# A fused attention and token-mixing kernel: q and k share each load tile on the two partition halves, in longer rows

One Trainium2 chip, one core. The metric is the device time in microseconds (us) of one execution, median over runs. "DMA us" below means packet time summed over all records of the trace and divided by the 16 DMA engines of the core.

Terms: PE is TensorE (matmuls and transposes), DVE VectorE, ACT ScalarE, POOL GpSimd, and SP issues the DMAs. HBM is the chip's main memory, SBUF the on-chip memory of 128 partitions, PSUM the memory that PE writes to; an eviction copies from PSUM to SBUF. A packet is one DMA record of the trace, here one contiguous row (8,192 of 2,304 B for q and k before, 4,096 of 4,608 B after). A transfer is full height when it stands on 128 partitions, half height on 64. Clash is my word for something that the traces show and do not explain: with half-height transfers on partitions 0 to 63 or 64 to 127, packets can take clearly longer than others of their size. In the kernel before, the last pair of half-height stores took 127 ns a packet of 2,048 B on average, the full-height weight loads of that size 84.6 ns. I call such packets stretched, and packets near the median of full-height transfers undisturbed (84 ns for 2,048 B, 93 for 2,304 B). An engine's part of a transfer is taken as a sixteenth of its packets. A run counts as slow when it is over 1.5% above the fastest of its kernel; ratios leave slow runs out.

## The reference

Eight batches of 8 heads, 576 tokens, 64 values a head: attention with a causal window of 128 tokens and a bias linear in distance, then a token mixer on the concatenated heads.

```python
scores = q @ k.T / 8 + slopes[h] * -(i - j)        # kept where 0 <= i - j < 128
attn   = softmax(scores) @ v                       # 8 x 8 x 576 x 64
x      = heads concatenated                        # 8 x 576 x 512
wq, wk = x @ w_q, x @ w_k                          # 512 -> 64
mixed  = (wq @ wk.T / 8) @ x
out    = relu(mixed) @ w_out                       # fp32, 8 x 576 x 512
```

q, k and v are fp32 in HBM, 9.4 MB each.

## The kernel before

Every operation is a small record, and a string, PLAN, lists the operations in order with engine and PSUM bank. All DMAs are issued from SP on one queue. The parts that matter here:

```python
RINGS = {"ld": 8, ..., "qT": 4, "kT": 4, ..., "osb": 3, ...}
ld = [sb([P, 2, 576], FP32, f"ld{i}") for i in range(8)]           # 128 partitions, rows of 2,304 B

# per batch b, group f of four heads, x = q or k: one load of 576 KB over 128 partitions
nc.sync.dma_start(out=t, in_=srcs[x][b].rearrange(
    "(f i a) (g j) d -> f (a g) i (j d)", f=2, a=2, j=9)[f])
copy(eng, n, t.rearrange("p i (j d) -> p j i d", j=9))             # cast to fp16, mostly on POOL
for j in range(9):                                                 # transposes on PE
    for a in range(2):
        r = slice(64 * a, 64 * a + 64)
        nc.tensor.transpose(bank(bk[a])...[:, 64 * j : 64 * j + 64], n[r, j]..., ident[r, r])
copy(eng, dst.rearrange("p a (g j) -> p a g j", j=9),              # eviction to qT or kT, contiguous
     src.rearrange("p a (j g) -> p a g j", j=9))
...                                                                # [cut] scores, exp, bias, values, mixer
nc.sync.dma_start(out=out[b, P*(t-1) : P*(t+1), :].rearrange("(p t) d -> p t d", t=2),
                  in_=osb[n % 3])                                  # stores of two tiles, 512 KB
```

The softmax here doesn't subtract the row's maximum and nothing guards it: scores larger than these inputs give would overflow.

## Time and profile before

| | before |
|---|---|
| time, median (range), 4 runs | 151.48 us (150.78 to 153.2) |
| span of the profiled run, granted clock | 149.7 us, 1.00 |
| busy PE, DVE, ACT | 125.7, 125.7, 118.5 us |
| DMA us, all records | 134.3 |
| of it packets of q and k (8,192 of 2,304 B) | 58.2, mean 113.6 ns, median 93 |
| of it packets of 256 B (v and the two small weights, 37,888) | 46.8, mean 19.8 ns, median 18 |

The prediction shows the lines of the page, of the table by stretch, of the chain and of the waits. One view is added: the page's list of DMA issues, which gives for each kind count, KB and median us from issue to landing.

```profile
ld<-in_k_dram SPq DMA_DIRECT2D x16, 576.0 KB, 6.9
ld<-in_q_dram SPq DMA_DIRECT2D x16, 576.0 KB, 7.0
```

And the place where the input stage ends, in the timeline of PE (start us, length us): the last 18 transposes of q and k.

```profile
118.07 0.44 PE L159 MATMUL bank<-ident,nat 64*128 64x64 f16 x18
```

From there to the end of the span are 149.7 - 118.1 = 31.6 us.

### The profile page before, as it was taken

The page shows a single profiled execution, that of the slowest core. Times are in us where ns is not written, and L with a number is a line of the kernel's source. Part 1 is how long each engine was busy: PE and PEld are TensorE (multiplying, and loading weights), DVE is VectorE, ACT ScalarE, POOL GpSimd, SP SyncE. Part 2 cuts the span into 40 slices and gives each one's busy share as a digit, 9 for nine tenths or more (in the row PEclk, how much of TensorE's full clock was granted, in tenths as well). Part 3 has the DMA queues.
Part 4 walks back from the last instruction along what each step waited for, and adds up shares of the span by engine and source line. Part 5 has one row for each costly group of instructions (what it writes and reads, how often), then busy time and mean ns, then how long its engine had stood idle before and what let it go on. Part 6 is the DMA issues. An engine that isn't in the chain of part 4 may idle for free.

```text
span 149.7 us, 5314 instructions
## 1 busy us (share of the span) xinstructions
PE 125.7 (84%) x2308; PEld 82.6 (55%) x2308; DVE 125.7 (84%) x212; ACT 118.5 (79%) x170; POOL 58.9 (39%) x78
## 2 busy tenths in 40 slices
PE   6567388676889979889989999999789999999870
PEld 6465167555756456547466566576544757555320
DVE  5749987979999998789999989999799989994700
ACT  6959937995889868997799999959889989741560
POOL 4064137354915767333845381364341710000000
PEclk9999999999999999999999999999999999999999
DMA  4999999999999999999999999799699896033075
GB/s 151 383 327 266 180 365 351 264 171 358 389 263 191 296 299 195 236 306 309 348 348 372 338 405 227 167 254 279 157 371 340 235 385 222 4 140 144 0 314 176
DMA packets 50775, 39.40 MB, mean 263 GB/s; under 512 B 39488, under 2 KB 39488, under 8 KB 50752
## 3 DMA queue, kind: packets, MB, share of 16 engines
q1 hardware_dynamic: 50752, 39.07, 88.7%
q8 instruction: 18, 0.29, 0.8%
q14 instruction: 5, 0.04, 0.1%
HBM read 29.62 MB, written 9.44 MB: 261 GB/s over the span
## 4 chain that ended last, share of the span: by engine, by line
PE 40%; DMA 16%; DVE 13%; ACT 12%; SPq 9%; POOL 4%; issue 2%; POOLq 0%; DVEq 0%
PE bank L159 40%; DMA ld<-in_q_dram 10%; SPq L159 9%; ACT pt L159 8%; DMA ld<-in_k_dram 6%; DVE pt L159 5%; POOL nat L159 2%; ACT qT L159 2%; DVE xT L159 2%; POOL vt L159 2%; DVE x L159 2%; ACT kT L159 1%; DVE kT L159 1%; DVE osb L159 1%; DVE rm L159 1%
## 5 line engine op out<-in xcount | busy, mean ns | idle before, releaser
L159 ACT ACTIVATE pt<-bank 128x1024 f16<-128x1024 f32 x64 | 62.7, 1036 | 9.3 <-PE bank L159 9.0
L159 POOL CAST nat<-ld 128x1152 f16<-128x1152 f32 x30 | 34.2, 1146 | 36.7 <-PE bank L159 10.6
L159 DVE TENSOR_TENSOR pt<-pt,table 128x2048 f16<-128x2048 f16 x32 | 41.0, 1293 | 2.1 <-ACT pt L159 2.0
L159 PE MATMUL bank<-wout_sb,rm 128*128 128x512 f16 x128 | 31.8, 380 | 0.0
L159 POOL CAST vt<-ldv 128x512 f16<-128x512 f32 (+1 forms) x35 | 20.8, 613 | 25.4 <-DVE pt L159 15.5
L159 PE MATMUL bank<-qT,kT 64*128 64x256 f16 (+2 forms) x320 | 25.4, 267 | 4.6 <-ACT qT L159 2.0
L159 PE MATMUL bank<-vt,pt 128*128 128x65 f16 x576 | 23.7, 200 | 4.6 <-ACT pt L159 3.1
L159 PEld LDWEIGHTS <-pt 128*128 128x128 f16 x576 | 21.4, 102 | 9.7 <-issue 2.6
L159 DVE TENSOR_TENSOR x<-bank,inv 128x640 f16<-128x640 f32 x32 | 25.8, 817 | 0.8
L159 PEld LDWEIGHTS <-kT 64*128 64x128 f16 x320 | 14.5, 99 | 11.5 <-issue 8.6
L159 ACT COPY osb<-bank 128x512 f32<-128x512 f32 x24 | 13.9, 606 | 7.1 <-PE bank L159 7.1
L159 PE MATMUL bank<-ident,nat 64*128 64x64 f16 x576 | 14.7, 199 | 5.6 <-POOL nat L159 2.8
L159 PEld LDWEIGHTS <-nat 64*128 64x128 f16 x576 | 12.2, 100 | 10.1 <-POOL nat L159 4.7
L159 PEld LDWEIGHTS <-rm 128*128 128x128 f16 x128 | 10.8, 98 | 12.6 <-issue 2.5
L159 ACT COPY qT<-bank 128x1152 f16<-128x1152 f16 x12 | 13.5, 1121 | 2.6 <-PE bank L159 2.6
L159 ACT ACTIVATE rm<-bank 128x512 f16<-128x512 f32 x21 | 12.7, 610 | 2.2 <-PE bank L159 2.2
L159 DVE COPY kT<-bank 128x1152 f16<-128x1152 f16 x8 | 10.8, 1354 | 3.2 <-PE bank L159 3.2
L159 DVE COPY xT<-bank 128x640 f16<-128x640 f16 (+1 forms) x32 | 12.5, 448 | 0.4 <-PE bank L159 0.4
L159 PE MATMUL bank<-x,wkn 128*64 128x512 f16 x80 | 10.1, 383 | 0.0
L159 PE MATMUL bank<-wqT,gm 64*128 64x256 f16 x64 | 8.4, 288 | 1.5 <-DVE wqT L159 0.6
L159 ACT COPY kT<-bank 128x1152 f16<-128x1152 f16 x8 | 9.1, 1138 | 0.5 <-PE bank L159 0.5
L159 DVE TENSOR_SCALAR rm<-bank 128x512 f16<-128x512 f32 x11 | 7.5, 684 | 2.3 <-PE bank L159 2.2
(45 smaller groups left out, 112.1 us busy)
## 6 DMA issues: line engine op xcount, KB each, us to landing
ld<-in_k_dram SPq DMA_DIRECT2D x16, 576.0 KB, 6.9
ld<-in_q_dram SPq DMA_DIRECT2D x16, 576.0 KB, 7.0
ldv<-in_v_dram SPq DMA_DIRECT2D x32, 256.0 KB, 7.1
out_dram<-osb SPq DMA_DIRECT2D x16, 512.0 KB, 5.2
ldv<-in_v_dram SPq DMA_DIRECT2D x8, 128.0 KB, 7.3
osb<-in_moe_w_out_dram SPq DMA_DIRECT2D x2, 512.0 KB, 7.1
out_dram<-osbt SPq DMA_DIRECT2D x8, 128.0 KB, 3.8
osbt<-in_moe_w_q_dram SPq DMA_DIRECT2D x1, 128.0 KB, 5.3
```

The source lines that it names most:

```text
L159: r = call(*a, **k)
```

## The change

The intent: rows of 18 tokens (4,608 B) halve the packets of q and k. So that a transposed group still holds two heads on each partition column, q then needs 64 partitions only; q takes partitions 0 to 63 of a tile, k 64 to 127. Besides: the last batch stores tile by tile, a fourth output buffer, more evictions allowed on ACT, and a new PLAN.

```diff
-    ld = [sb([P, 2, 576], FP32, f"ld{i}") for i in range(RINGS["ld"])]     # 8
+    ld = [sb([P, 2, 1152], FP32, f"ld{i}") for i in range(RINGS["ld"])]    # 4
-                    nc.sync.dma_start(out=t, in_=srcs[x][b].rearrange(
-                        "(f i a) (g j) d -> f (a g) i (j d)", f=2, a=2, j=9)[f])
+                    nc.sync.dma_start(out=t[64 * x : 64 * x + 64], in_=srcs[x][b].rearrange(
+                        "(f i a) (g j) d -> f (a g) i (j d)", f=2, a=2, j=18)[f])
-                    copy(eng, n, t.rearrange("p i (j d) -> p j i d", j=9))
+                    copy(eng, n, t.rearrange("p i (h j d) -> p h j i d", h=2, j=9)[:, h])
-                    copy(eng, dst.rearrange("p a (g j) -> p a g j", j=9),
-                         src.rearrange("p a (j g) -> p a g j", j=9))
+                    dst = qkT[b % 2][:, f, :, :, 0:S].rearrange(
+                        "p x a (g h j) -> p x a g h j", h=2, j=9)[:, :, :, :, h]
+                    copy(eng, dst, src[:, :, 0:S].rearrange("p x (j a g) -> p x a g j", j=9, a=2))
...                                                       # [cut] reads of qT, kT become reads of qkT
-            op({"DVE": 0.74}, f"XTe{b}{c}", ...           # likewise WKe, WQe
+            op({"DVE": 0.74, "ACT": 1.05}, f"XTe{b}{c}", ...
-"osb": 3
+"osb": 4
+            if b == NB - 1:                               # last batch: one store of 256 KB per tile
+                    nc.sync.dma_start(out=out[b, P * t : P * t + P, :],
+                                      in_=osb[n % RINGS["osb"]][:, t % 2, :])
...                                                       # [cut] PLAN replaced as a whole
```

More of the change, by code (lines that the diff above doesn't have):

```diff
@@ L99 @@
 PLAN = """
-1G 6D 39S 4D 0G 35S 2D 7D 47S 3G 8P0 5D 43S 14P0 20A 65S 19A 11P0 23A 59S 18A 12P0 17A 61S 24A 25D
-21A 9P0 57S 22A 40A 15P0 53S 26D 13P0 51S 10P0 55S 36A 41P2 73S 42D2 69S 37P0 31S 38A0 48G 33S
-250P0 99S 49P2 251A0 44G 245P4 91S 50D2 243P6 77S 244A6 45P0 248P2 66G 46D0 246A4 249A2 67P6 247D
-260P0 255P4 261A0 258P2 62G 68D6 60A 253P0 259A2 58D 63P6 252D 64A6 256A4 262D 254A0 52D 54D 56A
-257D 85S 403P0 95S 406P2 79S 404D0 74G 405D0 265P4 81S 263P6 266A4 407D2 83S 408D2 411P0 70G 87S
@@ L105 @@
-264A6 414P4 412D0 413D0 117S 75P2 32G 71P6 29S 415D4 34G 409P0 416D4 72A6 27S 410D0 113S 417P4
-76A2 268P6 100G 418D4 270P0 269A6 280P2 267D 101P4 281A2 273P6 92G 102D4 274A6 531P2 78G 271A0
-532D2 278P6 93P4 86G 275P2 279A6 272D 535P0 94A4 96G 533P1 536D0 276A2 534D1 80G 537P4 539P0 277D
-111S 97P2 538A4 16P6 125S 98A2 82G 540D0 109S 84G 105S 282D 103S 427P0 419P2 107S 88G 428D0 121S
-295P4 420D2 429D0 422P6 296A4 143S 421D2 293P0 118G 89P4 294A0 423D6 424D6 430P2 90A4 431D2 30G
-541P0 425P6 432D2 542A0 283P4 426D6 433P2 284A4 28G 288P0 434D2 285P6 286A6 297D 290P4 547P2 289A0
@@ L111 @@
-543P6 287D 545P3 544A6 300P0 114G 546D3 291A4 119P6 548D2 549P3 120D6 301A0 126G 298P4 550A3 115P0
-292D 127P6 299A4 650P2 110G 128D6 116A0 645P3 106G 651A2 112G 137S 557P0 646D3 553P4 104G 643P2
-139S 554A4 558D0 133S 108G 644A2 135S 302D 435P0 131S 438P2 129S 122G 436D0 310P4 439D2 440D2
-648P6 147S 311A4 647S 437D0 303P2 144G 649A6 123P4 304A2 124D4 138G 145P0 446P6 146A0 308P2 140G
-447D6 448D6 443P4 309A2 555P0 444D4 441P6 134G 445D4 556A0 141P2 142A2 442D6 449P0 305P4 136G
-450D0 306A4 551P6 313P2 552D6 559P0 314A2 132G 307D 315P4 163S 318P6 316A4 320P2 157S 655P1 130G
@@ L117 @@
-560D0 151S 319A6 451P4 159S 321A2 663P0 148G 195S 452D4 453D4 177S 323P6 664A0 312D 325P2 165S
-149P4 656A1 161S 563P0 324A6 322D 169S 326A2 561P1 155S 317D 652S 454P6 564A0 462P2 150A4 164G
-455D6 562D1 653P0 463D2 152G 456D6 459P4 654A0 464D2 660P1 160G 657S 460D4 158G 461D4 173S 153P2
-661A1 328P6 189S 154D2 658P0 329A6 196G 203S 330P4 191S 659D0 565P6 333P2 331A4 199S 566D6 178G
-457P0 334A2 465P4 458D0 197P6 466D4 198A6 338P0 166G 571P2 572D2 340P4 339A0 573P6 327D 341A4
-575P7 162G 574D6 335P0 569P2 567P4 336A0 170G 577P6 568D4 570A2 576D7 156G 179P0 578D6 167P2 180A0
@@ L123 @@
-171P4 332D 467P6 168A2 666P0 337D 172A4 668P1 468D6 469D6 470P2 667A0 669A1 579P4 471D2 581P6
-472D2 174G 580A4 673P0 670S 582A6 662S 585P2 342D 175P4 185S 586A2 345P6 671P1 346A6 183S 190G
-674D0 181S 478P2 204G 176A4 672D1 187S 348P6 479D2 207S 480D2 475P0 349A6 192G 350P4 476D0 583P2
-477D0 351A4 473P6 200G 474D6 481P0 584A2 343P4 482D0 344A4 353P6 355P2 352D 587P0 356A2 683P1
-588D0 354A6 347D 678P0 684A1 186G 193P2 679A0 358P4 194D2 360P6 359A4 591P0 184G 361A6 357D 215S
-201P2 205P4 209S 202A2 589P1 182G 592D0 221S 681P6 590D1 206A4 217S 188G 211S 362D 491P0 682A6
@@ L129 @@
-233S 483P2 225S 492D0 486P4 484D2 216G 493D0 676P6 208G 487D4 485D2 686P7 210G 677A6 488D4 680S
-597P0 687A7 370P2 598D0 213S 494P4 371A2 222G 675S 593P6 495D4 373P0 594A6 496D4 241S 489P2 374A0
-229S 380P6 490D2 218G 497P4 665S 498D4 381A6 223P2 375P0 212G 224D2 365P4 237S 376A0 601P6 235S
-366A4 603P7 602D6 685S 377D 363P0 239S 599P2 368P4 364A0 605P6 600D2 226G 369A4 604D7 595P0 606D6
-234G 227P2 596A0 219P4 372D 378P6 220A4 696P0 214G 228D2 379A6 694P1 697A0 367D 613P4 607P2 609P6
-608A2 689P0 610A6 382D 507P2 614A4 691P6 690A0 242G 508D2 509D2 695A1 499P4 230G 692A6 611P0 500D4
@@ L135 @@
-383P2 501D4 612A0 693S 502P6 384A2 688S 238G 231P0 503D6 504D6 510P4 232A0 698S 709P2 236G 511D4
-512D4 385P0 505P6 386A0 400P4 506D6 701P3 401A4 710D2 240G 398P0 702D3 513P6 711S 399A0 393P4
-514D6 699P2 394A4 402D 615P3 700A2 395P0 616D3 388P4 703S 396A0 390P6 387D 617P2 389A4 619P3 618D2
-397D 391A6 515P0 706P2 620A3 516D0 392D 621P4 625P6 622A4 704P3 517D0 707A2 626D6 518P4 705A3
-627P0 519D4 708S 523P6 520D4 628A0 623P2 524D6 526P0 624A2 525D6 521P4 527D0 528D0 714P2 522D4
-529P0 715A2 712P3 530D0 629P2 713D3 631P0 630D2 716S 633P1 632D0 717P0 634A1 639P2 637P4 635P6
@@ L141 @@
-640A2 638D4 641P2 636D6 719P1 642A2 718D0 727P2 720D1 729P3 728A2 721S 724P2 730A3 731S 722P3
-725A2 732P2 723A3 726S 733A2 734S
-"""
-RINGS = {"ld": 8, "ldv": 8, "nat": 6, "vt": 10, "qT": 4, "kT": 4, "P": 4, "x": 8, "xT": 8,
-         "wkn": 2, "wqT": 2, "g": 2, "rm": 8, "rmt": 8, "osb": 3, "osbt": 2, "inv": 3}
+1G 6D 36S 0G 2D 35S 7D 43S 5D 3G 11P0 4D 44S 12P0 19A 61S 23A 14P0 24A 18A 62S 21A 9P0 22A 59S 20A
+15P0 26D 17A 51S 10P0 55S 25D 8P0 53S 13P0 37G 40A 57S 69S 16P0 70S 38P2 41P0 39D2 42A0 48G 248P0
@@ new lines @@
+243P2 249A0 45G 49P4 245P6 244A2 50D4 46P0 246A6 250P2 47D0 63G 251A2 66G 64P4 60A 260P0 65D4
+258P2 261A0 52G 67P6 68A6 247D 253P0 255P4 259A2 56D 54D 254A0 262D 85S 58A 77S 252D 256A4 79S
+403P0 83S 265P2 404D0 257D 266A2 81S 406P4 33S 263P6 407D4 405D0 264A6 74G 87S 411P2 88S 412D2
+268P0 408D4 71G 75P6 31S 269A0 413D2 29S 270P4 76A6 96S 267D 72P0 414P2 95S 73A0 409P6 80G 415D2
+416D2 78G 111S 271A4 275P0 410D6 417P2 84G 27S 276A0 418D2 273P4 86G 114S 280P6 82G 113S 274A4
+278P2 272D 103S 419P0 281A6 109S 34G 420D0 107S 422P4 279A2 277D 531P6 105S 122S 423D4 532A6 421D0
@@ new lines @@
+427P2 121S 89G 535P6 428D2 424D4 32G 429D2 92G 533P7 536A6 90P0 534A7 282D 93P2 91A0 543P4 541P6
+94A2 30G 544D4 430P0 542A6 539P4 431D0 285P2 432D0 97G 286A2 283P6 540D4 425P0 284A6 100G 290P2
+426D0 433P4 291A2 434D4 98P6 28G 148S 537P0 538D0 147S 99A6 288P4 101P2 112G 129S 643P0 287D 102A2
+139S 140S 650P1 289A4 644D0 115G 131S 298P2 651D1 133S 295P6 299A2 116P4 104G 645P0 117D4 118G
+296A6 545P1 646A0 292D 300P2 546A1 119P4 293P6 301A2 547P0 108G 120D4 549P1 294A6 110G 106G 548D0
+648P2 550A1 302D 137S 135S 553P0 649A2 435P4 297D 165S 554A0 438P2 310P0 436D4 123G 439D2 437D4
@@ new lines @@
+443P6 311A0 444D6 440D2 126G 308P4 446P0 309A4 445D6 551P2 447D0 552A2 557P6 448D0 441P4 149G
+558A6 305P2 442D4 124P0 306A2 555P6 125D0 130G 127P4 556A6 449P2 152G 128A4 303P6 450D2 655P0
+304A6 312D 313P2 315P4 314A2 660P1 141G 656D0 316A4 559P0 307D 153P2 661A1 318P6 320P4 319A6 132G
+560D0 561P1 317D 163S 663P0 562A1 166S 321A4 134G 154D2 150P6 157S 563P1 151A6 138G 161S 136G
+664D0 647S 142P2 564A1 322D 155S 454P4 143A2 159S 569P0 451P6 164G 455D4 652S 570A0 456D4 459P2
+144G 173S 653P0 452D6 460D2 174S 453D6 170G 191S 145P4 461D2 565P6 146A4 192S 658P1 654D0 158G
@@ new lines @@
+167G 566A6 571P2 189S 659D1 325P4 326A4 183S 567P6 572D2 171P0 162G 199S 172D0 568A6 328P2 200S
+462P4 329A2 657S 457P6 463D4 323P0 464D4 662S 156G 668P2 324A0 185S 458D6 187S 465P4 669A2 160G
+330P0 466D4 340P6 181S 331A0 666P2 218S 327D 341A6 217S 338P4 168P0 209S 667D2 573P3 169A0 207S
+332D 467P6 339A4 671P2 468D6 574D3 333P0 672D2 178G 335P4 334A0 575P3 469D6 577P2 336A4 576D3 342D
+345P0 343P4 346A0 470P6 578D2 193G 673P3 471D6 344A4 472D6 175G 581P0 674A3 194P4 582D0 473P6
+195A4 585P2 190G 474D6 176P0 184G 586A2 177D0 348P4 196G 478P6 349A4 579P2 479D6 179P0 337D 580A2
@@ new lines @@
+583P4 584A4 350P2 201G 480D6 180A0 475P4 678P6 351A2 204G 476D4 477D4 202P0 679A6 353P2 481P4
+203A0 683P6 482D4 354A2 347D 360P0 358P4 681P7 361A0 684D6 188G 587P2 359A4 682D7 186G 197P0 588D2
+182G 355P6 205P4 356A6 352D 589P2 213S 670S 676P3 198A0 357D 211S 483P6 677A3 675S 486P0 206A4
+484D6 219G 215S 485D6 591P3 590A2 487D0 362D 220P4 592A3 365P6 221A4 686P2 210G 488D0 222G 241S
+491P0 366A6 687D2 225S 593P4 492D0 214G 597P2 226S 594A4 493D0 595P6 208G 596A6 363P4 599P0 239S
+598A2 600D0 494P6 237S 364A4 370P2 495D6 235S 689P0 496D6 212G 371A2 665S 367D 368P4 223P6 369A4
@@ new lines @@
+489P2 688S 694P1 490D2 216G 224A6 233S 372D 499P2 695A1 696P4 690A0 242G 500D2 501D2 385P6 502P0
+386A6 697D4 497P2 503D0 378P4 698S 504D0 227G 691P6 379A4 685S 498D2 680S 230G 373P0 505P4 692D6
+374A0 228P2 506D4 390P6 693S 240G 391A6 380P0 229D2 238G 603P4 381A0 601P5 236G 604D4 375P2 602D5
+388P0 376A2 383P6 382D 605P4 384A6 377D 510P2 606A4 231P6 389A0 234G 511D2 512D2 507P4 232A6 508D4
+609P0 509D4 611P2 610A0 612D2 613P6 513P4 614A6 607P0 514D4 393P2 608A0 395P6 387D 398P4 394A2
+615P0 396A6 699P1 392D 515P2 616A0 397D 399A4 400P6 617P0 401A6 516D2 619P4 517D2 618A0 402D 700A1
@@ new lines @@
+518P2 620A4 523P6 519D2 526P0 520D2 704P4 524D6 527D0 525D6 701P5 705A4 528D0 521P2 702D5 529P0
+522A2 621P6 530D0 706P4 703S 622D6 629P5 707A4 625P0 630D5 623P2 708S 627P6 624A2 631P4 628A6
+633P5 632D4 626A0 709P4 634A5 637P0 710A4 641P2 635P6 638D0 712P5 642A2 711S 636D6 639P0 714P4
+640A0 713A5 734P0 715A4 719P1 716S 735A0 736S 717P0 720A1 731P1 718A0 721S 728P0 732A1 733S 722P1
+729A0 730S 725P0 723A1 724S 726D0 727S
+"""
+RINGS = {"ld": 4, "ldv": 8, "nat": 6, "vt": 10, "qkT": 8, "P": 4, "x": 8, "xT": 8,
+         "wkn": 2, "wqT": 2, "g": 2, "rm": 8, "rmt": 8, "osb": 4, "osbt": 2, "inv": 3}
@@ L256, in steps @@
     vt = [sb([P, 5, 520], F16, f"vt{i}") for i in range(2)]
-    qT = [sb([P, 4, S], F16, f"qT{i}") for i in range(2)]
-    kT = [sb([P, 4, 640], F16, f"kT{i}") for i in range(2)]
+    qkT = [sb([P, 2, 2, 2, 640], F16, f"qkT{i}") for i in range(2)]
     pt = sb([P, 4, 2, 1088], F16, "pt")
@@ L267, in steps @@
     rmt = [sb([P, 4, P], F16, f"rmt{i}") for i in range(2)]
-    osb = [sb([P, 2, DM], FP32, f"osb{i}") for i in range(3)]
-    osbt = [sb([P, DM], FP32, f"osbt{i}") for i in range(2)]
+    osb = [sb([P, 2, DM], FP32, f"osb{i}") for i in range(RINGS["osb"])]
+    osbt = [sb([P, DM], FP32, f"osbt{i}") for i in range(RINGS["osbt"])]
     ident = sb([P, P], F16, "ident")
@@ L321, in f_kzero @@
         for i in range(2):
-            nc.vector.memset(kT[i][:, :, S:640], 0.0)
+            nc.vector.memset(qkT[i][:, :, 1, :, S:640], 0.0)
     def f_pads(eng, bk):
@@ L374, in steps @@
     for i in range(4):
-        r = [("osb", i - 3) if i < 2 else ("osbt", i - 4)]
+        r = [("osb", i - RINGS["osb"]) if i < 2
+             else ("osbt", i - 2 - RINGS["osbt"])]
         op({"SP": 0.6}, f"ld w{i}", (20, 20, 8, 8)[i], lambda eng, bk, i=i: f_ldw(eng, bk, i),
@@ L386, in steps, with f_cast, f_xpose @@
         for f in range(2):
+            i = 2 * b + f
+            t = ld[i % RINGS["ld"]]
+            base = b * PERIOD + 2 * f * SLOT
             for x in range(2):
-                i = 4 * b + 2 * f + x
-                t, n = ld[i % RINGS["ld"]], nat[i % RINGS["nat"]]
-                base = b * PERIOD + 2 * f * SLOT + 0.4 * x
                 def f_load(eng, bk, b=b, x=x, f=f, t=t):
-                    nc.sync.dma_start(out=t, in_=srcs[x][b].rearrange(
-                        "(f i a) (g j) d -> f (a g) i (j d)", f=2, a=2, j=9)[f])
-                def f_cast(eng, bk, t=t, n=n):
-                    copy(eng, n, t.rearrange("p i (j d) -> p j i d", j=9))
-                def f_xpose(eng, bk, x=x, n=n):
+                    nc.sync.dma_start(out=t[64 * x : 64 * x + 64], in_=srcs[x][b].rearrange(
+                        "(f i a) (g j) d -> f (a g) i (j d)", f=2, a=2, j=18)[f])
+                op({"SP": 0.6}, f"ld {'qk'[x]}{b}{f}", base - 14 + 0.4 * x, f_load,
+                   writes=[("ld", i)], dma=1.52)
+            for h in range(2):
+                n = nat[(2 * i + h) % RINGS["nat"]]
+                late = base + 0.4 * h
+                def f_cast(eng, bk, t=t, n=n, h=h):
+                    copy(eng, n, t.rearrange("p i (h j d) -> p h j i d", h=2, j=9)[:, h])
+                def f_xpose(eng, bk, n=n):
                     for j in range(9):
-                        for a in range(2):
-                            r = slice(64 * a, 64 * a + 64)
-                            o = bank(bk[a]).bitcast(F16)
+                        for x in range(2):
+                            r = slice(64 * x, 64 * x + 64)
+                            o = bank(bk[x]).bitcast(F16)
                             nc.tensor.transpose(o[:, 64 * j : 64 * j + 64],
@@ L406, in f_xpose, with f_evac @@
                                                 ident[r, r])
-                def f_evac(eng, bk, b=b, x=x, f=f):
-                    dst = (qT, kT)[x][b % 2][:, 2 * f : 2 * f + 2, 0:S]
-                    src = pairs[bk[0] // 2].bitcast(F16).rearrange("p (a w) -> p a w", a=2)[:, :, 0:S]
-                    copy(eng, dst.rearrange("p a (g j) -> p a g j", j=9),
-                         src.rearrange("p a (j g) -> p a g j", j=9))
-                name = f"{'qk'[x]}{b}{f}"
-                op({"SP": 0.6}, "ld " + name, base - 14, f_load, writes=[("ld", i)], dma=1.65)
+                def f_evac(eng, bk, b=b, f=f, h=h):
+                    dst = qkT[b % 2][:, f, :, :, 0:S].rearrange(
+                        "p x a (g h j) -> p x a g h j", h=2, j=9)[:, :, :, :, h]
+                    src = pairs[bk[0] // 2].bitcast(F16).rearrange("p (x w) -> p x w", x=2)
+                    copy(eng, dst, src[:, :, 0:S].rearrange("p x (j a g) -> p x a g j", j=9, a=2))
+                name = f"{b}{f}.{h}"
                 op({"POOL": 1.12} if b else {"POOL": 1.12, "DVE": 1.15, "ACT": 1.0},
-                   "cast " + name, base - 9, f_cast, reads=[("ld", i)], writes=[("nat", i)])
+                   "cast " + name, late - 9, f_cast, reads=[("ld", i)], writes=[("nat", 2 * i + h)])
                 key = "T " + name
-                op({"PE": 0.28}, key, base - 4, f_xpose, reads=[("nat", i), ("ident", 0)],
+                op({"PE": 0.28}, key, late - 4, f_xpose, reads=[("nat", 2 * i + h), ("ident", 0)],
                    opens=(key, 2), mode="R")
-                op({"ACT": 1.0, "DVE": 1.26}, "evac " + name, base - 3.5,
-                   f_evac, psum=key, reads=[("kzero", 0)] * x, writes=[(("qT", "kT")[x], 2 * b + f)])
+                op({"ACT": 1.0, "DVE": 1.26}, "evac " + name, late - 3.5, f_evac, psum=key,
+                   reads=[("kzero", 0)], writes=[("qkT", 2 * i + h)])
         for kb in range(5):
@@ L450, in f_scores @@
                             if kb < 4:
-                                kk = kT[b % 2][r, c, P * kb : P * kb + P]
+                                kk = qkT[b % 2][r, c // 2, 1, c % 2, P * kb : P * kb + P]
                                 w = 256 if kb < 3 else 192
                             else:
-                                kk, w = kT[b % 2][r, c, 512:640], 64
+                                kk, w = qkT[b % 2][r, c // 2, 1, c % 2, 512:640], 64
                             nc.tensor.matmul(ps[:, a : a + w], kk,
-                                             qT[b % 2][r, c, P * kb : P * kb + w],
+                                             qkT[b % 2][r, c // 2, 0, c % 2,
+                                                        P * kb : P * kb + w],
                                              start=True, stop=True)
@@ L465, in steps @@
                 op({"PE": 0.24}, key, base + 0.95 * u - 0.8, f_scores,
-                   reads=[("qT", 2 * b + c // 2), ("kT", 2 * b + c // 2)],
+                   reads=[("qkT", 4 * b + 2 * (c // 2) + h) for h in range(2)],
                    opens=(key, 2), mode="R")
@@ L542, in steps @@
                reads=[("x", n - 1), ("x", n), ("ident", 0)], opens=(key, 2), mode="R")
-            op({"DVE": 0.74}, f"XTe{b}{c}", prio + 2.0, f_xte, psum=key,
+            op({"DVE": 0.74, "ACT": 1.05}, f"XTe{b}{c}", prio + 2.0, f_xte, psum=key,
                reads=[("zero", 0)], writes=[("xT", n - 1), ("xT", n)])
@@ L582, in steps @@
            opens=(f"WK{b}", 1))
-        op({"DVE": 0.41}, f"WKe{b}", base + 3.0, f_wke, psum=f"WK{b}", writes=[("wkn", b)])
+        op({"DVE": 0.41, "ACT": 0.39}, f"WKe{b}", base + 3.0, f_wke, psum=f"WK{b}", writes=[("wkn", b)])
         op({"PE": 0.56}, f"WQ{b}", base + 4.0, f_wq, reads=r_xT + [("w", 2)],
            opens=(f"WQ{b}", 1), mode="C")
-        op({"DVE": 0.41}, f"WQe{b}", base + 4.5, f_wqe, psum=f"WQ{b}", writes=[("wqT", b)])
+        op({"DVE": 0.41, "ACT": 0.39}, f"WQe{b}", base + 4.5, f_wqe, psum=f"WQ{b}", writes=[("wqT", b)])
         op({"PE": 1.1}, f"G{b}", base + 4.0, f_g, reads=r_x + [("wkn", b)],
@@ L624, in f_out @@
                 for db in range(4):
-                    r = slice(256 * (t // 2) + t % 2, 256 * (t // 2) + 256, 2)
+                    r = (slice(256 * (t // 2) + t % 2, 256 * (t // 2) + 256, 2) if b < NB - 1
+                         else slice(P * t, P * t + P))
                     nc.tensor.matmul(bank(bk[0]), rm[:, b % 2, db, r],
@@ L629, in f_oute @@
             def f_oute(eng, bk, t=t, n=n):
-                copy(eng, osb[n % 3][:, t % 2, :], bank(bk[0]))
+                copy(eng, osb[n % RINGS["osb"]][:, t % 2, :], bank(bk[0]))
             key = f"O{b}{t}"
@@ L635, in steps, with f_store @@
             op({"ACT": 0.49, "DVE": 0.62}, f"Oe{b}{t}", base + t * SLOT + 1.0, f_oute, psum=key,
-               writes=[("osb", n)])
-            if t % 2:
+               writes=[("osb", n)] + [(f"last{t}", 0)] * (b == NB - 1))
+            if b == NB - 1:
+                def f_store(eng, bk, b=b, t=t, n=n):
+                    nc.sync.dma_start(out=out[b, P * t : P * t + P, :],
+                                      in_=osb[n % RINGS["osb"]][:, t % 2, :])
+                op({"SP": 0.6}, f"st{b}{t}", base + t * SLOT + 1.6, f_store, dma=0.75,
+                   reads=[(f"last{t}", 0)])
+            elif t % 2:
                 def f_store(eng, bk, b=b, t=t, n=n):
@@ L640, in f_store @@
                         out=out[b, P * (t - 1) : P * (t + 1), :].rearrange("(p t) d -> p t d", t=2),
-                        in_=osb[n % 3])
+                        in_=osb[n % RINGS["osb"]])
                 op({"SP": 0.6}, f"st{b}{t}", base + t * SLOT + 1.6, f_store, dma=1.45,
@@ L652, in f_outte @@
             def f_outte(eng, bk, pr=pr):
-                copy(eng, osbt[pr % 2], bank(bk[0]))
+                copy(eng, osbt[pr % RINGS["osbt"]], bank(bk[0]))
             def f_storet(eng, bk, pr=pr):
@@ L657, in f_storet @@
                     nc.sync.dma_start(out=out[2 * pr + i, 512:576, :],
-                                      in_=osbt[pr % 2][64 * i : 64 * i + 64])
+                                      in_=osbt[pr % RINGS["osbt"]][64 * i : 64 * i + 64])
             key = f"OT{pr}"
```

## The prediction

The rival of heavy clashes came to 156 to 163 us, from up to 14 us more of DMA work for q and k (72 us, 282 ns a packet), with up to 60% of the packets taken as stretched. Three figures can be set beside the traces. The fit of 0.0366 ns per byte and 9 ns is an estimate from the medians of two sizes; it gives 18.4 and 93.3 ns for 256 and 2,304 B, where the medians are 18 and 93. At most 8 transfers were in flight, from issue to landing, in the traces of both kernels. The pair of xT evictions on ACT, 1.3 us by estimate, took 0.69 + 0.59 us after the change.

> **What bounds the kernel now.** I read the busy shares first, then the stretches of 15 us, then the chain that ended last, then the DMA queue and the waits behind it. The first two lines are the page's, the rest the table by stretch (stretch, length, then busy us and instruction count of each engine, granted clock, DMA share, GB/s).
>
> ```profile
> PE 125.7 (84%) x2308; PEld 82.6 (55%) x2308; DVE 125.7 (84%) x212; ACT 118.5 (79%) x170; POOL 58.9 (39%) x78
> ...
> q1 hardware_dynamic: 50752, 39.07, 88.7%
> ...
> 0.00:15.00 15.00, 9.89 (x158) 8.14 (x159) 10.08 (x23) 11.82 (x17) 5.74 (x13) 1.00 0.95 282
> 15.00:30.00 15.00, 10.13 (x234) 8.25 (x234) 13.02 (x21) 11.62 (x15) 6.20 (x8) 1.00 1.11 290
> 30.00:45.00 15.00, 11.56 (x259) 8.94 (x260) 13.52 (x22) 12.07 (x17) 7.87 (x10) 1.00 1.03 295
> ...
> 90.00:105.00 15.00, 14.44 (x299) 9.58 (x299) 14.40 (x26) 12.99 (x20) 6.26 (x10) 1.00 0.92 229
> 105.00:120.00 15.00, 13.75 (x240) 8.09 (x234) 14.02 (x21) 13.75 (x23) 6.29 (x9) 1.00 0.93 279
> 120.00:135.00 15.00, 15.00 (x257) 9.26 (x257) 14.42 (x28) 11.29 (x18) 0.62 (x1) 1.00 0.49 183
> 135.00:150.00 15.00, 9.52 (x72) 4.30 (x70) 4.32 (x9) 4.93 (x10) 0.00 (x0) 1.00 0.42 158
> ```
>
> There is no single bound. Until 45 us the DMA engines are full (shares 0.95 to 1.11) and PE is busy only 31.6 of 45 us: loads bound this part. From 45 to 135 us PE has 84.6 and DVE 83.8 of 90 us, and until 120 us the DMA share is still above 0.9: three resources are near their end together, and a gain in one can be swallowed by the next. The granted clock is 1.00 throughout. The chain of waits in order of time (start us, us, what) says when the loads let go:
>
> ```profile
> 100.48 8.88 DMA ld<-in_q_dram
> ...
> 109.51 1.16 POOL nat L159
> ...
> 110.72 27.95 PE bank L159 x454
> ...
> 139.45 5.61 PE bank L159 x26
> ...
> 145.09 0.58 ACT osbt L159
> ```
>
> A q load issued at 100.5 lands at 109.4; from 110.7 PE works for 28 us without a wait, then 5.6 us of output projections, one eviction, stores, end at 149.7. What brings the last q and k in earlier, or shortens those last us, shortens the kernel. Issue to landing is 6.9 to 7.0 us for q and k, so several transfers queue ahead of each. What the load queue and the casts wait for:
>
> ```profile
> SPq L159 <- ACT osb L159: 13.0, 5, 5.3
> SPq L159 <- DVE osb L159: 10.4, 2, 5.5
> ...
> POOL nat L159 <- DMA ld<-in_q_dram: 10.1, 8, 3.4
> POOL nat L159 <- DMA ld<-in_k_dram: 9.4, 7, 5.4
> ```
>
> The casts of q and k waited 19.5 us for loads. The 23.4 us on osb are stores that wait for their eviction, with loads stuck behind them in the queue; no line has an eviction waiting for a store to leave its buffer.
>
> I also averaged the trace's DMA packet records by size. 256 B: 37,888 packets, median 18 ns, mean 19.8. 2,048 B: 1,024, 84 and 94.4. 2,304 B (q and k): 8,192, 93 and 113.6. 4,096 B (paired stores): 2,048, 159 and 162.1. All records sum to 2.149 ms, over 16 engines 134 us: q and k are 8192 x 113.6 / 16 = 58.2 us of it, v and the small weights 46.8, stores of pairs 20.7.
>
> [...](159 - 84) / 2048 = 0.0366 ns per byte and 9 ns fixed, from the medians.
> [...]The kernel before has two kinds of half-height transfer. [...]The tail stores of 2,048 B do tell: the last pair, alone on the queue, averages 127 ns with many packets at 140 to 165, against 84. But two of the four pairs, in the middle of other traffic, ran at 85.1 and 85.5. So the clash is real here[...].
>
> **The change, part by part.**
> *Loads of q and k.* 32 transfers of 576 KB stay, now 64 partitions high in rows of 4,608 B: 4,096 packets instead of 8,192. Undisturbed, 9 + 4608 x 0.0366 = 178 ns each, 4096 x 178 / 16 = 45.6 us against 8192 x 93 / 16 = 47.6: 2.0 us saved. Before, waiting added 113.6 - 93 = 20.6 ns to a packet, 10.5 us in all. If that goes with the bytes, the saving is 2.1 us; if it goes with the packets, 4096 x 198.6 / 16 = 50.8 us, a saving of 7.4. That is without clashes.
> *First use.* A cast now needs q and k of its group, but both its halves can start together, on ACT and POOL; before, the first two casts stood behind each other on ACT (5.1 and 6.1 us). About even.
> *Casts, transposes, score matmuls.* Same counts and shapes (32, 576, 320). The eviction to qkT writes runs of 9 elements at every second place; its PSUM source was strided before too:
>
> ```profile
> L159 ACT COPY qT<-bank 128x1152 f16<-128x1152 f16 x12 | 13.5, 1121 | 2.6 <-PE bank L159 2.6
> ...
> L159 DVE COPY kT<-bank 128x1152 f16<-128x1152 f16 x8 | 10.8, 1354 | 3.2 <-PE bank L159 3.2
> ```
>
> I take the same 1,121 to 1,138 ns on ACT and 1,354 on DVE.
> *Who evicts.* The instruction order of the two builds gives, for DVE: big q/k evictions 12 to 11 (-1.4), osb 8 to 13 (+3.4), osbt +1 (+0.7), gm -3 (-2.1), v casts -1 (-0.4), wkn -3 and wqT -4 (-3.4), one xT pair (-0.9), one relu pair (-0.9): -5.0 us, to about 121. ACT: big evictions 20 to 21 (+1.1), osb -5 (-3.0), osbt -1 (-0.6), gm +3 (+1.8), wkn and wqT +7 at about 0.45 (+3.1, an estimate between its 239 ns for 64 columns and 606 for 512), xT +1.3 (estimate), relu +0.85, nat cast -1.1: +3.4, to about 122. DVE was the fuller engine and carries 13% of the chain, 19 us; 4% off that is 0.8 us.
> *Last stores.* The old end issues a 512 KB store and then two tail stores (1.1 us of issue); landings 147.5, 148.0 and 148.6. The new order ends with one 256 KB store. Its last eviction starts at the same point after PE, so only one issue and some queueing goes: 0.5 us.
> *Fourth output buffer.* As no eviction waited for a store, 0 directly; it only gives the new order freedom.
>
> The sum without clashes: loads 2 to 7 us less DMA work, of which I let half reach the end, because the engines have only 5 to 6 us of slack in 45 to 135: 1 to 3.7. With 0.8 and 0.5, 2.3 to 5.0 off 152.2: 147.2 to 149.9.
>
> **The rivals.**
> [...]A clash stretches 2,048 B from 84 to about 150 ns; scaled, 178 becomes 318. If all packets clash, q and k take 4096 x 318 / 16 = 81 us, 23 more than now. Break-even with the present 227 ns for 4,608 B, with 20 ns of waiting kept, is (227 - 198) / 140, about 20% clashing. [...]As loads bound the first part, most of it would arrive: 156 to 163. Against: half of the tail pairs clashed hardly at all, and all 512 tail packets average 104 ns, 31% of the way to 150; [...]and the diff lowers the scheduler's figure for such a load from 1.65 to 1.52 us, which looks like a measured one, though I can't verify it.
> *The loads get quicker and nothing follows.* PE at 94% and DVE at 93% of 45 to 135 take over: 150.5 to 152, what remains being tail and balance.
> *The order is worse on the chip than in its planner.* A pair shares one ring slot of 4 in place of 2 of 8, so a buffer comes free only after two casts; with 8 transfers in flight this could hold up loads for a us or two: 152 to 154.
>
> **Range and chances.** I give the sum without serious clashes a bit over half, centred near 148.3; moderate clashes or swallowed gains (150 to 155) about a quarter; heavy clashes (155 to 164) a fifth or more. The median of this mixture is 149.3. The range 145.8 to 158.0 leaves out the heaviest clashes. The limits of 2% are 149.1 and 155.2: faster 0.43, within 0.33, slower 0.24.
>
> **What would show it.** Right: 4,608 B packets of 180 to 225 ns on average, the DMA share before 45 us unchanged but PE busier there than 31.6 us, the last q or k load landing by 107 us, qkT evictions within 3% of the times above, DVE and ACT both near 122 us. Wrong: a second heap of packets at 300 ns or more, landings later than 7.0 us, PE idle on loads beyond 45 us (heavy clashes); or evictions to qkT clearly longer than 1,138 and 1,354 ns, which I'd have missed altogether.

## More of the kernel before

Entries of q and k are about 0.1, so scores are about 0.01 and hardly move the softmax. This matters for the experiments: a kernel that mixes up the heads of q and k still agrees with the reference within its tolerance. Where I call a layout correct, I evaluated the program functionally, off the chip, on inputs with q and k 12 times as large, for which a swap shows: relative error (rms) 0.0008 for the kernels before and after, about 1 for a scrambled one.

## The result, and the profile after

187.25 us (186.26 to 187.46, 4 runs; of two more one was slow, 190.37) against 151.48: ratio 1.237, 95% interval 1.229 to 1.246. Ratios here are the mean time of one kernel's fast runs over that of the other's in the same rounds, so they differ a little from the ratio of the medians quoted.

The page's busy shares and its DMA queue, after:

```profile
PE 136.7 (74%) x2308; PEld 87.5 (47%) x2308; DVE 122.1 (66%) x202; ACT 126.1 (68%) x178; POOL 63.6 (34%) x80
...
q1 hardware_dynamic: 46944, 39.07, 95.8%
```

The same bytes, 8% fewer packets, and yet the queue was full for a larger share of a longer span. The table by stretch, with the columns of the prediction's first fence:

```profile
15.00:30.00 15.00, 8.92 (x168) 6.85 (x168) 10.26 (x12) 9.81 (x12) 4.42 (x5) 0.52 1.10 206
30.00:45.00 15.00, 10.34 (x210) 7.69 (x206) 11.74 (x20) 9.89 (x11) 7.43 (x9) 0.77 1.11 221
...
105.00:120.00 15.00, 10.37 (x170) 6.56 (x168) 9.63 (x17) 9.11 (x14) 5.58 (x6) 0.82 1.06 230
...
135.00:150.00 15.00, 13.04 (x224) 7.90 (x224) 11.23 (x22) 11.81 (x17) 6.25 (x9) 0.89 1.11 249
150.00:165.00 15.00, 14.20 (x281) 9.89 (x276) 14.65 (x24) 13.62 (x21) 2.04 (x4) 1.00 0.54 182
```

The DMA engines are full until 150 us, at 206 to 230 GB/s in the first three of these rows, where before it was 279 to 295 in the same three. PE and DVE, at 92 to 93% from 105 to 120 us before, are now busy two thirds of that stretch: the kernel is load-bound until about 150 us. In the chain that ended last, DMA and the load queue (SPq) have grown from 25% to 56% of the span (first before, then after):

```profile
PE 40%; DMA 16%; DVE 13%; ACT 12%; SPq 9%; POOL 4%; issue 2%; POOLq 0%; DVEq 0%
```
```profile
DMA 31%; PE 26%; SPq 25%; ACT 6%; DVE 4%; POOL 4%; issue 2%; POOLq 0%
```

The issues, the waits of the casts, and the last transposes of q and k say the same:

```profile
ld<-in_k_dram SPq DMA_DIRECT2D x16, 576.0 KB, 9.8
ld<-in_q_dram SPq DMA_DIRECT2D x16, 576.0 KB, 9.0
```
```profile
POOL nat L159 <- DMA ld<-in_k_dram: 34.3, 9, 8.9
...
POOL nat L159 <- DMA ld<-in_q_dram: 17.5, 4, 6.4
```
```profile
154.60 0.44 PE L159 MATMUL bank<-ident,nat 64*128 64x64 f16 x18
```

The casts on POOL waited 51.8 us for q and k instead of 19.5. The last transposes come 154.6 - 118.1 = 36.5 us later, and from there to the end it is 184.6 - 154.6 = 30.0 us instead of 31.6. So the whole loss of 34.9 us of span lies before the last q and k are in; what follows is a little faster than before.

The packet records (averaged as in the prediction) show where the added DMA time lies:

| | packets of q and k | mean, median ns | DMA us | 256 B mean ns | DMA us | all records, DMA us |
|---|---|---|---|---|---|---|
| before | 8,192 of 2,304 B | 113.6, 93 | 58.2 | 19.8 | 46.8 | 134.3 |
| after | 4,096 of 4,608 B | 337.8, 346 | 86.5 | 24.9 | 58.9 | 178.7 |

Of 44.4 us more, 28.3 are q's and k's own, 12.1 are the 256 B packets that run beside them, the rest (4.0) other stores, weights and completions. 82% of the 4,608 B packets took 300 ns or more; only 8% took 200 or less.

### The profile page after: what moved, and what is told of

Read it like the earlier page. It is cut to its first block, busy times and chain, and to the rows that moved or that the text cites. A ratio compares the mean times of both kernels' runs of the same rounds, so it can differ in the third digit from the quotient of the medians.

```text
span 184.6 us, 5327 instructions
## 1 busy us (share of the span) xinstructions
PE 136.7 (74%) x2308; PEld 87.5 (47%) x2308; DVE 122.1 (66%) x202; ACT 126.1 (68%) x178; POOL 63.6 (34%) x80
## 4 chain that ended last, share of the span: by engine, by line
DMA 31%; PE 26%; SPq 25%; ACT 6%; DVE 4%; POOL 4%; issue 2%; POOLq 0%
PE bank L159 26%; SPq L159 25%; DMA ld<-in_q_dram 19%; DMA ldv<-in_v_dram 12%; ACT pt L159 3%; POOL nat L159 3%; ACT qkT L159 2%; DVE osb L159 1%; DVE xT L159 1%; DVE rm L159 1%; POOL vt L159 1%; ACT rm L159 1%; DVE x L159 0%; ACT gm L159 0%; DVE vt L159 0%
## 5 line engine op out<-in xcount | busy, mean ns | idle before, releaser
L159 ACT COPY qkT<-bank 128x1152 f16<-128x1152 f16 x21 | 26.7, 1282 | 19.5 <-PE bank L159 19.5
L159 PE MATMUL bank<-ident,nat 64*128 64x64 f16 x576 | 17.4, 211 | 29.8 <-POOL nat L159 23.4
L159 PE MATMUL bank<-wout_sb,rm 128*128 128x512 f16 x128 | 34.3, 402 | 2.0 <-POOL wout_sb L159 2.0
L159 PEld LDWEIGHTS <-nat 64*128 64x128 f16 x576 | 13.9, 108 | 36.5 <-POOL nat L159 29.3
L159 PE MATMUL bank<-qkT 64*128 64x256 f16 (+2 forms) x320 | 27.8, 289 | 2.5 <-ACT qkT L159 1.4
L159 DVE COPY qkT<-bank 128x1152 f16<-128x1152 f16 x11 | 14.8, 1355 | 13.6 <-PE bank L159 13.6
L159 PEld LDWEIGHTS <-qkT 64*128 64x128 f16 x320 | 15.8, 106 | 11.0 <-issue 6.0
L159 DVE COPY osb<-bank 128x512 f32<-128x512 f32 x13 | 8.9, 686 | 13.1 <-PE bank L159 13.0
L159 ACT COPY osb<-bank 128x512 f32<-128x512 f32 x19 | 11.2, 602 | 4.4 <-PE bank L159 4.3
L159 DVE RECIPROCAL inv<-bank 128x10 f32<-128x10 f32 x32 | 6.7, 214 | 10.3 <-PE bank L159 10.1
L159 PE MATMUL bank<-wqT,gm 64*128 64x256 f16 (+1 forms) x64 | 10.0, 327 | 1.2 <-ACT qkT L159 0.6
```

Source lines behind the costliest of these rows:

```text
L159: r = call(*a, **k)
```

## The experiments

Theory: the loads clash because each transfer stands on partitions 0 to 63 or 64 to 127 alone (4,608 B: mean 338 ns in the changed kernel, against an estimate of 178 undisturbed). In the expectations its name and its supposed cause are cut, as no run shows the cause; the figures that follow a cut are those of this theory. Rivals: rows over 4,096 B are slow (4,096 B were the longest rows that the kernel before moved, with a median of 159 ns); the new order, the coarser buffers or the eviction cost the time; any transfer of half height is slow; more or smaller transfers are.

**Full height, everything else kept.** The result is scrambled on purpose, as in the next one.

```diff
-                    nc.sync.dma_start(out=t[64 * x : 64 * x + 64], in_=srcs[x][b].rearrange(
-                        "(f i a) (g j) d -> f (a g) i (j d)", f=2, a=2, j=18)[f])
+                    nc.sync.dma_start(out=t[:, x], in_=srcs[x][b].rearrange(
+                        "(f h) (g j) d -> f (h g) (j d)", f=2, j=18)[f])
```

> The changed kernel with one edit: each q or k load spreads its 576 KB over all 128 partitions in the same rows of 4,608 B (128 rows, 8 packets an engine, as before the edit), so that q fills one half of each partition's row and k the other. The data land in the wrong places: the result is wrong on purpose, nothing else in the program changes, order and evictions included. [...]4,608 B packets fall from a mean of 338 ns to 180 to 225 ns, DMA records in all from 179 to about 130 us of 16 engines, the time to 146 to 152 us, the granted clock back near 1.00. Rival, rows over 4,096 B are slow in themselves: packets stay near 340 ns and the time near 187 us. Rival, the new order, the paired buffers or the strided eviction are to blame: packets get faster but the time stays above 165 us. In any case the eviction to qkT on ACT should stay at 1,282 ns if its strided destination is what makes it longer.

149.03 us (148.82 to 150.12) against 152.46 of the kernel before in these rounds: ratio 0.976 (0.972 to 0.979). Packets of 4,608 B: mean 200 ns, median 178, the figure that the prediction worked out. All records 132.3 DMA us. The casts' waits for q and k in the list of waits:

```profile
POOL nat L159 <- DMA ld<-in_q_dram: 4.1, 1, 4.1
...
POOL nat L159 <- DMA ld<-in_k_dram: 2.7, 2, 1.7
```

6.8 us instead of 51.8. The row length, the order, the paired buffers and the strided eviction are all still in, so none of them makes the loss. The granted clock rose from 0.847 to 0.954; I come back to it.

**Half height, short rows.**

```diff
+                        out=t[64 * x : 64 * x + 64].rearrange("p i (r n) -> p (i r) n", r=2),
+                        in_=srcs[x][b].rearrange("(f h) (g j) d -> f g h (j d)", f=2, j=9)[f])
```

> The changed kernel with one edit: the loads stay 64 partitions high, but in rows of 2,304 B (4 rows a partition, 16 packets an engine), which again puts the data in wrong places on purpose. [...]packets of 2,304 B at about 165 to 180 ns, near twice the 93 of the kernel before, and the time as slow as the change, 183 to 193 us. Row length theory: packets near 114 ns and the time 150 to 158 us.

188.86 us, ratio 1.237 (1.230 to 1.245), as slow as the change. Packets of 2,304 B: mean 171 ns, median 176, against 113.6 and 93. Row length is out as the cause.

**The kernel before, its loads cut in two**, once by height and once by rows. Both keep a correct result.

```diff
-                    nc.sync.dma_start(out=t, in_=src)
+                    for half in range(2):                      # e3_split_height
+                        r = slice(64 * half, 64 * half + 64)
+                        nc.sync.dma_start(out=t[r], in_=src[r])
+                    for i in range(2):                         # e4_split_rows
+                        nc.sync.dma_start(out=t[:, i], in_=src[:, i])
```

> The kernel before, correct, with one edit: every q or k load is issued as two transfers, one for partitions 0 to 63 and one for 64 to 127, the same rows of 2,304 B, the same layout, order, evictions. 32 transfers more, half as large. [...]packets of 2,304 B go from 114 to 165 ns or more, the time to 170 to 190 us, the granted clock falls below 0.95. Rivals that blame rows, order, buffers or evictions of the changed kernel: packets near 114 ns, the time as in the split by rows (e4_split_rows), within 2%.

> The control of e3_split_height: the kernel before, correct, every q or k load issued as two transfers, each over all 128 partitions with one of the two rows. Same number and size of transfers and packets as e3_split_height. All theories: packets of 2,304 B near 114 ns and granted clock 1.00; the time 150 to 157 us, what is over 151.5 being the price of 32 more transfers with 8 in flight. If it is as slow as e3_split_height, the number of transfers and not their height is what costs.

By height: 178.2 us (177.33 to 178.91), ratio 1.167 (1.161 to 1.173), packets mean 153 ns, median 156. By rows: 153.44 us (150.73 to 157.48), packets mean 112.3, median 93; three of its four runs, the profiled one among them, count as slow runs, so there is no ratio, and its one fast run of 150.73 lies with the kernel before; even its slowest run is about 20 us under the fastest of the split by height. The issues of the two (first by height, then by rows, the latter from a slow run):

```profile
ld<-in_k_dram SPq DMA_DIRECT2D x32, 288.0 KB, 7.6
ld<-in_q_dram SPq DMA_DIRECT2D x32, 288.0 KB, 7.0
```
```profile
ld<-in_k_dram SPq DMA_DIRECT2D x32, 288.0 KB, 5.5
ld<-in_q_dram SPq DMA_DIRECT2D x32, 288.0 KB, 5.6
```

The same number and size of transfers, the same rows; which rows one transfer brings, and so the partitions that it covers, differ. In the old kernel half height alone costs some 26 us (178.2 against 152.46 of the kernel before in the same rounds). The packets were 153 ns and not 165 or more as I expected, and the clock 0.945, at the edge of what I expected. Here an engine needs 8 x 93 = 0.74 us for its part of a transfer, half as long as in the change, and 63% of the packets were stretched (140 ns or more, 1.5 times the undisturbed 93) instead of 82% (300 ns or more). Why fewer were stretched, no run shows.

**The same half height on other partitions.** k is loaded full height, q half height; the place of q's 64 partitions differs. With it move the cleared parts: eight clears on DVE, done at 14.0 us, on 32 to 95, and four, done at 8.7 us, on 0 to 63, which works against 32 to 95. The reads from HBM are the same.

```diff
-                        nc.sync.dma_start(out=t[0:64, 1:3], in_=q[b]...      # g1_q_on_0_63
+                        nc.sync.dma_start(out=t[32:96, 1:3], in_=q[b]...     # g2_q_on_32_95
```

> The clash measured by itself, with q half-height and k full-height (data in wrong places on purpose). The changed kernel with a third row in each load tile: k is loaded as in e1_full_height over all 128 partitions into row 0, q is loaded 64 partitions high on partitions 0 to 63 into rows 1 and 2, all in rows of 4,608 B; both casts read rows 0 and 1 of all partitions (the part that q does not fill is cleared once at the start). [...]two heaps of 4,608 B packets, the half of them that is k near 180 to 200 ns, the half that is q near 340; time between e1_full_height and the change, 160 to 175 us. Rival, that a transfer of 64 partitions is slow wherever it stands: the same here, but then g2_q_on_32_95 is as slow.

> g1_q_on_0_63 with one edit: the 64 partitions of q are 32 to 95 instead of 0 to 63 (and the cleared part moves with it). Still 64 partitions, the same transfers, packets, order. [...]one heap of packets near 180 to 215 ns and a time of 147 to 153 us. Rival, height as such: packets of q near 340 ns and the time of g1_q_on_0_63.

On 0 to 63: 180.71 us (179.06 to 182.64; its profile is of the slowest run, which counts as slow). On 32 to 95: 158.54 (158.13 to 160.18). The issues, first on 0 to 63, then on 32 to 95:

```profile
ld<-in_k_dram SPq DMA_DIRECT2D x16, 576.0 KB, 10.0
ld<-in_q_dram SPq DMA_DIRECT2D x16, 576.0 KB, 9.7
```
```profile
ld<-in_k_dram SPq DMA_DIRECT2D x16, 576.0 KB, 6.9
ld<-in_q_dram SPq DMA_DIRECT2D x16, 576.0 KB, 7.4
```

Packets of 4,608 B: mean 315 ns, median 327, against mean 206, median 178. So height as such costs next to nothing: 206 ns here, 200 at full height in e1_full_height. Where the 64 partitions lie decides; why it does, the runs do not show. Two of my numbers were off. On 0 to 63 only half of the packets are half height, yet 58% took 300 ns or more, with a tail past 500: so at least 8 of these 58 points are full-height packets of k, which are stretched too, and the time is 181 and not 160 to 175. On 32 to 95 the time is 158.5, not 147 to 153. The start is held up, by the clears named above and, as I read it, a buffer that I had to share to make room; the stretch from 15 to 30 us of this kernel shows PE at 7.0 us and an idle queue:

```profile
15.00:30.00 15.00, 7.00 (x130) 5.82 (x130) 12.54 (x15) 9.34 (x11) 3.30 (x3) 1.00 0.47 135
```

**Everything but the loads.** The change with the old full-height loads, casts and evictions; correct.

```diff
+                        out=t[:, x].rearrange("p (i n) -> p i n", i=2),
+                        in_=srcs[x][b].rearrange(
+                            "(f i a) (g j) d -> f (a g) i (j d)", f=2, a=2, j=9)[f])
+                    copy(eng, n, t[:, h].rearrange("p (i j d) -> p j i d", i=2, j=9))
+                    dst = qkT[b % 2][:, f, h, :, 0:S].rearrange("p a (g j) -> p a g j", j=9)
```

> The changed kernel with its loads, casts and evictions of q and k put back as in the kernel before (128 partitions high, rows of 2,304 B, q and k in one tile side by side, contiguous eviction), and everything else of the change kept: the new order, the new share of evictions between ACT and DVE, last stores by tile, a fourth output buffer. Correct result. [...]2,304 B packets near 114 ns, time 147 to 152 us, granted clock near 1.00; against e1_full_height the difference is what rows of 4,608 B are worth, 0 to 4 us, and the eviction to qkT on ACT drops from 1,282 to 1,121 to 1,138 ns. Rival, the order or the buffers are to blame: 165 us or more.

Result: 150.26 us (148.97 to 151.71) against 152.59; ratio 0.994 (0.985 to 1.003). As that did not settle it, once more with other rounds:

> e5_after_full_rows9 again, beside e8_full_height_rows18 on the same chip and with the same runs of the kernel before, as its first interval (0.985 to 1.003) did not settle whether it beats the kernel before. Expected 0.98 to 0.995 of the kernel before.

150.1 us (149.37 to 150.89) against 151.86: ratio 0.993 (0.987 to 0.999). A gain of 0.7%. The profile of e5_after_full_rows9 is of a slow run, so figures of this kernel are taken from e9_full_rows9_again. The eviction of q and k on ACT, in the groups of the changed kernel and of this one (count, busy us, mean ns):

```profile
L159 ACT COPY qkT<-bank 128x1152 f16<-128x1152 f16 x21 | 26.7, 1282 | 19.5 <-PE bank L159 19.5
...
L159 DVE COPY qkT<-bank 128x1152 f16<-128x1152 f16 x11 | 14.8, 1355 | 13.6 <-PE bank L159 13.6
```
```profile
L159 ACT COPY qkT<-bank 128x1152 f16<-128x1152 f16 x21 | 23.4, 1135 | 7.0 <-PE bank L159 7.0
```

Runs of 9 elements at every second place cost ACT 147 ns for 1,152 elements (1,295 in e1_full_height, which keeps them); DVE takes 1,355 and 1,352.

**The small parts alone.** Four output buffers in the kernel before:

```diff
-"osb": 3
+"osb": 4
```

> The kernel before with four output buffers in place of three and nothing else; correct. My prediction gave it 0 us: within 0.5% of the kernel before. If stores held evictions up after all, 1 to 2 us less.

153.19 us (152.36 to 157.45) against 152.59, ratio 1.014 (1.006 to 1.022). Seven of the eleven runs of the kernel before in these rounds count as slow and are left out of the ratio, and they lie at 152.4 to 155.3, around this kernel's times. So I read it as no gain; whether there is a small loss stays open.

Stores by tile in the kernel before, last batch:

```diff
+            if b == NB - 1:
+                    nc.sync.dma_start(out=out[b, P * t : P * t + P, :], in_=osb[n % 3][:, t % 2, :])
```

> The kernel before with the stores of the last batch tile by tile, each just behind its eviction in the same order; correct. My prediction gave the new end 0.5 us (0.3%); here the two tail stores still come last, so 0 to 0.5 us less. A gain of over 1 us would mean the queue in front of the last store mattered more than I took it to.

150.97 us (150.65 to 152.35), ratio 1.003 (0.994 to 1.012): nothing to be seen at this resolution, as expected.

**A correct version with long rows at full height.** From the second batch on, a tile holds q alone or k alone of all 8 heads, and heads c and c + 4 share a partition column:

```diff
+                    if b:
+                        src = srcs[f][b].rearrange("(x h) (g j) d -> x (h g) (j d)", x=2, j=18)[x]
+                        nc.sync.dma_start(out=t[:, x], in_=src)
+                        dst = qkT[b % 3][:, :, f, :, 0:S].rearrange(
+                            "p y a (g h j) -> p y a g h j", h=2, j=9)[:, :, :, :, h]
...                                        # [cut] head numbers, PLAN: q and k half a batch earlier
```

> A correct version with the long rows and without the clash, checked by hand on inputs with q and k 12 times as large, for which a swap of heads shows. From the second batch on a tile holds q alone or k alone of all 8 heads, loaded by two transfers of 128 partitions (4 heads of 32 rows of 18 tokens); the two heads that share a partition column are c and c + 4. The first batch keeps rows of 9 tokens so that it can start early. The order is that of the change, with the loads, casts, transposes and evictions of q and k moved half a batch earlier, as a batch now needs all four casts before its first scores; a third buffer for the transposed q and k. If length of row at full height is what e1_full_height gained, 148 to 151 us, at or under e5_after_full_rows9; if the coarser tiles cost more than the rows give, 152 to 158 us.

155.46 us (154.86 to 157.51), ratio 1.028 (1.021 to 1.035): slower. Its packets are as hoped (4,608 B: mean 198 ns; all records 131.1 DMA us), but the stretch from 15 to 30 us has lost. The extra loads and casts were squeezed in there; that they are the cause is likely but was not tested:

```profile
15.00:30.00 15.00, 6.95 (x124) 5.26 (x121) 8.87 (x11) 7.80 (x9) 3.56 (x5) 0.50 1.03 261
```

PE at 6.95 us instead of 10.13 in the kernel before. The gain to be had from long rows is smaller than that: e1_full_height at 0.976 and e9_full_rows9_again at 0.993 of their kernels before are 1.8% apart, or 149.03 and 150.1 us, in different rounds and on different chips. A searched order might keep some of it; I did not find one. The best correct version here is therefore e5_after_full_rows9 (run again as e9_full_rows9_again), about 1 us under the kernel before.

## Why the prediction was wrong

**The step that failed** is the weighing of the clashes. The prediction had their break-even of 20% and their full price, and then gave heavy ones "a fifth or more" of the chances, on three grounds. Ground one, that two of four pairs of tail stores ran at 85 ns in the middle of other traffic: an engine's part of such a store is by estimate 4 x 84 ns = 0.34 us, that of a load in the change 8 x 178 ns = 1.4 us even undisturbed. A short transfer that escapes says little of a long one: of the 512 packets of all tail stores 28% were stretched (126 ns or more, 1.5 times 84), in e3_split_height, which lies between (0.74 us), 63%, in the change 82%. In order of their start the four pairs average 85, 88, 117 and 127 ns, so one of the three pairs amid other traffic clashed as well. Ground two, on how the loads of q and k follow each other, would have spared most packets, and 82% at 300 ns or more speak against that. Ground three, the scheduler's 1.52 us for such a load: at 338 ns a packet the chip takes 8 x 338 = 2.7 us. A number written in a program is not a measurement of that program. The prediction's own signs of being wrong came true: the second heap of packets, landings at 9.0 and 9.8 us, casts idle on loads far beyond 45 us, and longer evictions on ACT (not on DVE).

**The size was too low even for heavy clashes.** "If all packets clash" gave 318 ns and 81 us for q and k; measured were 338 and 86.5. And I gave the clash no effect on others: the 256 B packets rose from 19.8 to 24.9 ns, 12.1 DMA us more, which fell back to 20.7 ns in e1_full_height. So my heavy rival ended at 164 us where the chip took 187.

**How DMA time reaches the end.** "As loads bound the first part, most of it would arrive" held: 44.4 DMA us more became 34.9 us of span, all of it before the last q and k. The loads bound the changed kernel to about 150 us; the prediction had them bind the old one to 45.

**What the clash hid.** Without it my sum was 147.2 to 149.9 us; e1_full_height, which is the change without the clash, took 149.03. Of the parts: 178 ns for an undisturbed 4,608 B packet, right to the ns. Long rows saving 2 to 7 DMA us of q and k: 58.2 in the kernel before against 51.2, so 7.0, the upper end; but with the new order and short rows e9_full_rows9_again has 54.3, so the rows themselves are 3.1 of it, and all records fell by 2.0 only, from 134.3 to 132.3. DVE near 121 and ACT near 122 us: 120.8 and 121.6 in e9_full_rows9_again. The eviction to qkT on ACT, taken at 1,121 to 1,138 ns, was 1,282: 21 x 0.15 = 3 us of ACT that I missed because I looked at the strided source and not at the destination. The fourth buffer and the last stores, 0 and 0.5 us, are compatible with the runs but too small to be shown. The rival of the coarser buffers is out: they are in e1_full_height.

**The clock.** The granted clock of the profiled run is 0.847. By stretch it is 0.52 from 15 to 30 us, where PE was busy 8.9 of 15 us, and 1.00 from 150 to 165 us, where PE was busy 14.2. That the late loads brought the low clock is my reading and is not shown; no run held the clock up under the clash, so its own share isn't measured. An estimate bounds it: PE's busy time rose from 125.7 to 136.7 us, so slower matmuls can account for at most about 11 of the 34.9 us. Small differences in the clock figure mean little here, as the table shows 1.00 where the trace has no clock record. The trace of the kernel before has none until 24.1 us; 18 transposes took 0.66 to 0.70 us there up to 16 us, as in the changed kernel where its column shows 0.50 (0.66 at 21.0 us), and 0.43 to 0.44 from 27.6 us on. The prediction's "1.00 throughout" is wrong for the start, then, and so is the 1.00 shown for g2_q_on_32_95 from 15 to 30 us, whose records begin at 34.7 (18 transposes took 0.68 to 0.71 us there); the 0.954 of e1_full_height, whose records begin at 5.8 us, need not be a lower clock at all.

**What stays open** is what stretches the packets, and how it reaches full-height ones (at least 8 of 58 points in g1_q_on_0_63); the records do not name the engine of a packet. The landings do not settle it: from 30 to 120 us the 16 parts of a transfer land with a median standard deviation of 0.29 to 0.44 us in the three stretches of 30 us, against 0.41 to 0.60 in the kernel before.

## What to carry to other kernels

Before changing how a load is laid out, look at which partitions one transfer covers, not only how many packets it has. Here 128 partitions, or 64 that start at 32, ran at 200 and 206 ns a packet; 0 to 63 and 64 to 127 at 338. If a clash looks possible, find in the trace a transfer that is as long per engine as the planned one before you trust that it will be dodged. And count what a slower transfer does to the packets beside it: here those of 256 B went from 19.8 to 24.9 ns.
